# Beginning the stationary operand's tiles at 0, 64, 128 or 192 bytes from the moving operand's, modulo 256, in some visits of a two-matmul feed-forward

## The chip, the cores and the metric

One core of one Trainium2 chip runs the whole program. The metric is the device time of one execution in microseconds; the median of the runs counts. The program uses TensorE (PE; its weight loads are shown apart as PEld), VectorE (DVE), ScalarE (ACT), GpSimd (POOL) and the DMA queue of SyncE (SP).

## The reference

```python
scores = where((rel >= 0) & (rel < 64), q @ k.T / 8, -1e9)   # batch 8, heads 8, 576 positions, 64 wide
x = (softmax(scores) @ v)  ->  4608 tokens x 512
h = x @ w_in                                  # w_in 512 x 2048
g = maximum(h, 0) + alpha * minimum(h, 0)
out = g @ w_out                               # w_out 2048 x 512
```

All arrays are float32.

## The kernel before

The program has an early part and a late part. The early part is the banded attention in tiles of 128 tokens, and the first matmul with w_in, unit by unit of 512 tokens (n = 0 to 8); its g goes out to a scratch in DRAM. The late part, the function `second`, reads g back in quarters and forms the product with w_out by a scheme of Strassen's kind: of four quarters a11, a12, a21, a22 it takes seven sums (numbered by ORDER = 1, 2, 6, 7, 5, 3, 4), multiplies each with a prepared sum of w_out's quarters, and adds the seven products up at the end. There are 9 units times 4 duos of this (u = 0 to 35), so 252 products. One product is called a visit here.

The products are made to nearly float32 precision from two rounded parts of each operand, a high and a low one: high times high, high of g times low of w, low of g times high of w. For each visit ACT writes the high part of g's sum (`ys.u.i.h`, tile yh), DVE subtracts it from the sum to get the low part (`ys.u.i.l`, tile yl), and then PE issues twelve matmuls (`O.u.i`, L721): three pairs of parts, two halves j of the inner dimension, two halves h of the tokens. Each has a stationary operand of 128 columns, a slice of yh or yl, and a moving operand of 256 columns, a slice of wh or wl:

```python
for part, w in ((y_hi, w_hi), (y_hi, w_lo), (y_lo, w_hi)):
    for j in range(2):
        for h in range(2):
            nc.tensor.matmul(banks[bank][:, h * EH:(h + 1) * EH],
                             part[x][:, j * HW + h * P:j * HW + (h + 1) * P],   # stationary: g's sums
                             w[k][:, j * EH:(j + 1) * EH], ...)                 # moving: w_out's sums
```

PE loads the stationary slice of the next matmul while the present matmul streams its moving slice, so both read the same memory, SBUF, at the same time.

yh and yl exist ten times (SLOTS); `new_slot` hands them out in turn, so visit number v of the late part, counted in the order of the program from 0, uses slot v modulo 10.

A planner (`Program.order`) fixes the order of all instructions from costs and due times that are numbers in the code; the tiles' addresses play no part in it.

Where the tiles lie within a partition matters for the change. wh and wl (28 tiles of 512 float32 each) lie in one pool, one behind the other, and so do x's parts xh and xl of the even units (2,048 float32 each), diff, the partial sums and the cells. All these sizes are multiples of 2,048 bytes, so all these tiles begin at the same place modulo 2,048. The pool of the late part follows, and begins at that place too. It opens with a filler, `apart`, of 464 float32 (1,856 bytes, which is seven times 256 and 64 more). Behind it lie yh_0, yl_0, yh_1, yl_1 and so on, and then the tiles for g, 2,048 bytes each. So every yh, yl and g tile begins 64 bytes behind w's tiles modulo 256 (and 320 modulo 512). The slices that the matmuls take begin at multiples of 512 bytes within a tile. In the first matmul (`cell`, L625) the stationary operand is a slice of wh or wl and the moving one a slice of xh or xl; both begin at multiples of 512 bytes in tiles that begin at the same place, so there the two are 0 bytes apart modulo 256. Its unit n = 0 is partly done in halves, with 256 moving columns instead of 512.

Of the kernel before, what the change touches and what calls it, by code (L numbers as in the profile page):

```python
# [9 lines left out]
F32 = mybir.dt.float32  # L10
F32R = mybir.dt.float32r
# [3 lines left out]
ALU = mybir.AluOpType  # L15
# [166 lines left out]
def banded_attention_then_prelu_ffn(  # L182
# [11 lines left out]
    nc = tc.nc  # L194
    P = 128
# [11 lines left out]
    HW = BT * P // 2  # L207
    EH = E // 2
# [11 lines left out]
    w_hi, w_lo = ([const.tile([P, 512], F32R, name=f"w{x}_{k}") for k in range(7 * DUOS)] for x in "hl")  # L220
# [30 lines left out]
    banks = [psum.tile([P, 512], F32, name=f"bank_{i}") for i in range(6)]  # L251
# [8 lines left out]
    def halves_of(*bs):  # L260
        return [f"bank.{b}.{i}" for b in bs for i in range(2)]
# [3 lines left out]
    def add(name, engine, busy, emit, *args, **kw):  # L265
        p.add(name, {engine: (busy, emit)}, *args, **kw)
# [52 lines left out]
    raw_at = [0]  # L319

    def chunk(name, c, f, second, start=0.0):
        r = raw_at[0] % len(raws)
        ulps, k_ulps = ulp_ring[raw_at[0] % 2], f"e.ulps.{raw_at[0] % 2}"
# [100 lines left out]
    def bank_of(i):  # L424
        return banks[i].rearrange("p (e k) -> p e k", e=NP)
# [56 lines left out]
    def value(t, i):  # L482
        av = [bank_of(b).rearrange("p (i a) q -> p i a q", i=2)[:, i] for b in V_BANK]
        pt, at = turned[t % 2].rearrange("p a h u b q -> p a h (u b q)"), 2 * (t % KRING)
        for a in range(2):
            for block, to, from_ in ((1, slice(0, P), slice(W, 3 * W)), (0, slice(0, W), slice(0, W)),
                                     (2, slice(W, P), slice(3 * W, 4 * W))):
                for h in range(2):
                    for x in range(2):
                        r, hs = slice(x * W, (x + 1) * W), slice(h * D, (h + 1) * D)  # L490
                        nc.tensor.matmul(av[x][hs, a, to], vring[r, a, at + block, hs], pt[r, a, h, from_],  # L491
                                         start=block == 1, stop=block == 2)
# [110 lines left out]
    def begin_of(n):  # L603
        return BEGIN + n * CELL * NF
# [35 lines left out]


    y_hi, y_lo, ring = [], [], {"at": 0}

    def new_slot():
        ring["at"] += 1
        return (ring["at"] - 1) % SLOTS

    def fetch_weights(k):
        for at, (kept, key) in enumerate(((w_hi, f"wh.{k}"), (w_lo, f"wl.{k}"))):
# [3 lines left out]
    SETS, SLOTS = 4, 10  # L653
    g_of = []

    def open_late():

        early.close()
        pool = ctx.enter_context(tc.tile_pool(name="late", bufs=1))
        pool.tile([P, 464], F32, name="apart")  # L660
        for i in range(SLOTS):
            y_hi.append(pool.tile([P, 512], F32R, name=f"yh_{i}"))
            y_lo.append(pool.tile([P, 512], F32R, name=f"yl_{i}"))
        g_of.extend([pool.tile([P, 512], F32, name=f"g_{s}_{q}") for q in range(4)] for s in range(SETS))

    bank_ring, slot_of = [0], {}

    def y_keys(x):
        return [f"yh.{x}"], [f"yl.{x}"]

    def second(n):
        acc = {}
        for i in ORDER:
            acc[i] = bank_ring[0] % 8
            bank_ring[0] += 1
        for d in range(DUOS):
            u = n * DUOS + d
            s = u % SETS
            base = begin_of(NB) + 4.0 + u * UNIT
            for q in range(4):  # L680
                add(f"gf.{u}.{q}", "SP", 0.5, lambda s=s, q=q, d=d: nc.sync.dma_start(g_of[s][q].rearrange("p (j t) -> p j t", j=2), hidden[n][d][:, q]),
                    ["late", *(f"far.g.{n}.{d}.{q}.{j}" for j in range(2))], [f"g.{s}.{q}"], service=0.9, earliest=base - 45)

            def cell(q, s=s):
                return lambda: g_of[s][q]

            def both(name, to, a, b, op, reads, writes):
                add(name, "DVE", 0.61, lambda: nc.vector.tensor_tensor(out=to(), in0=a(), in1=b(), op=op), reads, writes)  # L688

            def parts(i, value, ks):  # L690
                x = slot_of[u, i] = new_slot()
                his, los = y_keys(x)
                add(f"ys.{u}.{i}.h", "ACT", 0.54, lambda: nc.scalar.copy(y_hi[x], value()), [*ks, "late"], his)  # L693
                add(f"ys.{u}.{i}.l", "DVE", 0.61, lambda: nc.vector.tensor_tensor(out=y_lo[x], in0=value(), in1=y_hi[x].bitcast(F32), op=ALU.subtract),  # L694
                    [*ks, *his], los)

            a11, a12, a21, a22 = (cell(q) for q in range(4))
            k11, k12, k21, k22 = ([f"g.{s}.{q}"] for q in range(4))
            d_ = lambda: diff
            parts(1, a11, k11)  # L700
            parts(2, a12, k12)
            both(f"z3.{u}", d_, a11, a21, ALU.subtract, [*k11, *k21], ["diff"])
            both(f"z1.{u}", a21, a21, a22, ALU.add, k22, k21)
            both(f"z2.{u}", a11, a21, a11, ALU.subtract, k21, k11)
            parts(6, a11, k11)
            parts(7, d_, ["diff"])
            parts(5, a21, k21)
            both(f"z4.{u}", a12, a12, a11, ALU.subtract, k11, k12)
            parts(3, a12, k12)
            parts(4, a22, k22)  # L710
            for at, i in enumerate(ORDER):
                x, bank = slot_of[u, i], acc[i]

                k = 7 * d + at

                def emit(k=k, x=x, bank=bank, d=d):
                    done = 0
                    for part, w in ((y_hi, w_hi), (y_hi, w_lo), (y_lo, w_hi)):
                        for j in range(2):
                            for h in range(2):  # L720
                                nc.tensor.matmul(banks[bank][:, h * EH:(h + 1) * EH], part[x][:, j * HW + h * P:j * HW + (h + 1) * P],  # L721
                                                 w[k][:, j * EH:(j + 1) * EH], start=d == 0 and not done,
                                                 stop=d == DUOS - 1 and done == 11, skip_group_check=True)
                                done += 1

                add(f"O.{u}.{i}", "PE", STEP, emit, [f"wh.{k}", f"wl.{k}", *y_keys(x)[0], *y_keys(x)[1]], halves_of(bank), key=base + at * STEP)

        def total(name, to, k_to, r, i):
            add(name, "DVE", 0.6, lambda: nc.vector.tensor_tensor(out=to, in0=banks[acc[i]], in1=sums_of[r], op=ALU.add),
                [*halves_of(acc[i]), f"r.{r}"], k_to)  # L730

        def write(m, y, cell):
            at = (n * BT + m * BT // 2) * P
            to = out[at:at + HW, y * EH:(y + 1) * EH].rearrange("(i p) e -> p i e", p=P)
            add(f"out.{n}.{m}.{y}", "SP", 0.5, lambda: nc.sync.dma_start(to, cells[cell].rearrange("p (i e) -> p i e", i=2)),
                [f"cell.{cell}.0", f"cell.{cell}.1"], [], service=0.9)

        add(f"u1.{n}", "ACT", 0.5, lambda: nc.scalar.copy(sums_of[0], banks[acc[1]]), halves_of(acc[1]), ["r.0"])
        total(f"d11.{n}", cells[0], ["cell.0.0", "cell.0.1"], 0, 2)
        write(0, 0, 0)  # L740
        total(f"u2.{n}", sums_of[1], ["r.1"], 0, 6)
        total(f"u3.{n}", sums_of[2], ["r.2"], 1, 7)
        total(f"d22.{n}", cells[3], ["cell.3.0", "cell.3.1"], 2, 5)
        write(1, 1, 3)
        total(f"u4.{n}", sums_of[0], ["r.0"], 1, 5)
        total(f"d12.{n}", cells[1], ["cell.1.0", "cell.1.1"], 0, 3)
        write(0, 1, 1)
        total(f"d21.{n}", cells[2], ["cell.2.0", "cell.2.1"], 2, 4)
        write(1, 0, 2)
# [26 lines left out]
    for k in range(KEPT, 7 * DUOS):  # L776
        fetch_weights(k)
    odd_x = [key for c in range(NP) for part in ("xh", "xl") for key in x_keys(part, 4 + c)]
    add("late", "POOL", 0.0, open_late, (), [*early_keys, *odd_x, "late"])
    for n in range(NB):  # L780
        second(n)
# [49 lines left out]
```

## Time and profile before

| | us |
|---|---|
| median of 3 runs | 869.62 (868.14 to 870.24) |
| the profiled execution, its time | 872.26 |
| its span in the trace | 870.5 |
| PE busy | 856.1 (98%) |
| DVE busy | 686.5 (79%) |
| ACT busy | 441.6 (51%) |
| POOL busy | 203.6 (23%) |

The span is the time from the first to the last instruction of the trace; the profiled execution's own time is 1.8 us longer. Busy PE time counts matmuls that overlap, each with an end that is modelled, so the pace of PE is read from the starts of its matmuls, not from their lengths.

### The profile page before, as it was taken

The numbers are of one execution on the slowest core, as the hardware profiler recorded it, in microseconds if no ns is written. First come the engines' busy times: TensorE is split into PE (matmuls) and PEld (weight loads), VectorE is DVE, ScalarE is ACT, GpSimd is POOL, SyncE is SP. The second block draws the span as 40 slices with busy tenths as digits, with TensorE's granted clock in tenths as the row PEclk, the third lists the DMA queues.
The fourth block names the chain that finished last, engine by engine and source line by source line (L and its number), as shares of the span: only waits on it lengthen the run. The fifth ranks groups of instructions, "written<-read, shape, count | busy, mean of one in ns | idle before, by whom it ended". The sixth has DMA issues, their size and how long they took to land.

```text
span 870.5 us, 21140 instructions
## 1 busy us (share of the span) xinstructions
PE 856.1 (98%) x7888; PEld 772.7 (89%) x7888; DVE 686.5 (79%) x1755; ACT 441.6 (51%) x1118; POOL 203.6 (23%) x192
## 2 busy tenths in 40 slices
PE   7999999999999999999999999999999999999998
PEld 7888888888788787888888899999999999999998
DVE  3967899968987897898685547978788887978783
ACT  4887656564467545545434334444444444444441
POOL 3878525762127327411100000000000000000000
PEclk9999999999999999999999999999999999999999
DMA  6888656644468757755326995545444444545201
GB/s 193 246 257 271 211 185 212 200 155 156 158 223 269 257 160 267 243 173 161 113 98 195 319 339 175 156 120 151 119 137 123 145 135 121 151 117 158 83 27 49
DMA packets 121271, 152.91 MB, mean 176 GB/s; under 512 B 10576, under 2 KB 92496, under 8 KB 121168
## 3 DMA queue, kind: packets, MB, share of 16 engines
q1 hardware_dynamic: 120896, 151.30, 55.0%
q8 instruction: 62, 1.02, 0.5%
q14 instruction: 41, 0.34, 0.1%
q10 hardware_dynamic: 272, 0.26, 0.1%
HBM read 95.95 MB, written 55.57 MB: 174 GB/s over the span
## 4 chain that ended last, share of the span: by engine, by line
PE 72%; DVE 11%; DMA 7%; ACT 4%; issue 3%; POOL 2%; SPq 0%; POOLq 0%; DVEq 0%; ACTq 0%
PE bank L721 41%; PE bank L625 25%; DMA raw<-w_out 4%; DVE pt L468 3%; DVE cell L632 3%; ACT w L451 2%; PE bank L491 2%; DVE pt L470 2%; PE bank L435 2%; DMA wol<-staged 1%; PE bank L293 1%; DVE w L444 1%; PE bank L475 1%; DMA raw<-w_in 1%; ACT cell L631 1%
## 5 line engine op out<-in xcount | busy, mean ns | idle before, releaser
L693 ACT CAST yh<-g 128x512 fp32r<-128x512 f32 x216 | 133.3, 622 | 149.9 <-PE bank L721 98.5
L631 ACT ACTIVATE cell<-bank,alphas 128x512 f32<-128x512 f32 (+1 forms) x148 | 99.7, 674 | 163.0 <-PE bank L625 158.8
L694 DVE TENSOR_TENSOR yl<-g,yh 128x512 fp32r<-128x512 f32 x216 | 147.7, 688 | 30.5 <-ACT yh L693 28.5
L625 PE MATMUL bank<-xh,wh 128*128 128x512 f32 (+1 forms) x592 | 160.7, 393 | 3.3 <-DVE cell L632 2.9
L721 PE MATMUL bank<-wl,yh 128*128 128x256 f32 x1008 | 160.0, 281 | 0.0
L721 PE MATMUL bank<-wh,yh 128*128 128x256 f32 x1008 | 160.0, 281 | 0.0
L721 PE MATMUL bank<-wh,yl 128*128 128x256 f32 x1008 | 160.0, 281 | 0.0
L632 DVE SCALAR_TENSOR_TENSOR cell<-bank,alphas,cell 128x512 f32<-128x512 f32 (+1 forms) x148 | 108.1, 734 | 63.0 <-ACT cell L631 56.0
L625 PE MATMUL bank<-xl,wh 128*128 128x512 f32 (+1 forms) x592 | 155.5, 385 | 0.8 <-DVE xl L559 0.7
L625 PE MATMUL bank<-xh,wl 128*128 128x512 f32 (+1 forms) x592 | 155.0, 384 | 0.0
L721 PEld LDWEIGHTS bank<-wl,yh 128*128 128x128 f32 x1008 | 137.5, 190 | 0.0
L721 PEld LDWEIGHTS bank<-wh,yh 128*128 128x128 f32 x1008 | 136.5, 189 | 0.2
L721 PEld LDWEIGHTS bank<-wh,yl 128*128 128x128 f32 x1008 | 136.4, 189 | 0.0
L625 PEld LDWEIGHTS bank<-xh,wh 128*128 128x128 f32 x592 | 106.0, 188 | 31.1 <-DVE cell L632 9.6
L625 PEld LDWEIGHTS bank<-xl,wh 128*128 128x128 f32 x592 | 109.5, 188 | 23.8 <-DVE xl L559 1.2
L625 PEld LDWEIGHTS bank<-xh,wl 128*128 128x128 f32 x592 | 109.6, 188 | 22.1
L451 ACT ACTIVATE w<-w,nm 128x128 f32<-128x128 f32 x288 | 112.0, 393 | 28.4 <-DVE nm L444 28.2
L460 POOL TENSOR_TENSOR w<-w,rc 128x512 f32<-128x512 f32 x72 | 75.2, 1063 | 140.3 <-DVE rc L456 126.2
L468 DVE STREAM_TRANSPOSE pt<-w 32x256 f32<-32x256 f32 x184 | 80.1, 435 | 7.4 <-POOL w L460 4.4
L688 DVE TENSOR_TENSOR g<-g,g 128x512 f32<-128x512 f32 x108 | 74.2, 687 | 2.4 <-DMA g<-g 0.6
L444 DVE CUSTOM_DVE_ANT_0 w<-bank,masks 128x128 f32<-128x128 f32 x288 | 63.5, 285 | 12.0 <-PE bank L435 11.9
L470 DVE STREAM_TRANSPOSE pt<-w 32x128 f32<-32x128 f32 x184 | 55.7, 303 | 3.8
(62 smaller groups left out, 706.9 us busy)
## 6 DMA issues: line engine op xcount, KB each, us to landing
g<-g SPq DMA_DIRECT2D x144, 256.0 KB, 3.4
g<-cell SPq DMA_DIRECT2D x140, 256.0 KB, 2.9
out<-cell SPq DMA_DIRECT2D x36, 256.0 KB, 2.5
q<-qT SPq DMA_DIRECT2D x35, 256.0 KB, 6.1
raw<-w_in SPq DMA_DIRECT2D x16, 512.0 KB, 5.0
raw<-w_out SPq DMA_DIRECT2D x16, 512.0 KB, 6.5
k<-kT SPq DMA_DIRECT2D x18, 384.0 KB, 5.0
v<-vN SPq DMA_DIRECT2D x18, 384.0 KB, 5.8
```

The lines of the kernel that those rows point to most:

```text
L444: nc.vector.tensor_tensor_reduce(out=of_head(weights[t % 2], g), in0=bank_of(S_BANK[t % 2][x])[:, e].rearrange("p (b k) -> p b k", b=2), i ...
L451: nc.scalar.activation(w, w, AF.Exp, scale=-1.0, bias=least[t % 2][:, g:g + 1], accum_out=sums[:, t % 2, g, 0:1])
L460: nc.gpsimd.tensor_tensor(out=w, in0=w, in1=rc.unsqueeze(1).unsqueeze(3).broadcast_to(list(w.shape)), op=ALU.mult)
L468: nc.vector.transpose(to, w[:, x, j])
L470: nc.vector.transpose(to[:, :, j ^ 1], w[:, x, j, :, j ^ 1])
L625: nc.tensor.matmul(h, w[KEPT + f][:, a * P:(a + 1) * P], v[:, a, half], start=k == a == 0, stop=k == 2 and a == NP - 1, skip_group_check=True)
L631: add(f"sl.{name}", "ACT", 0.13 + 0.46 * part, lambda: nc.scalar.activation(g, h, AF.Copy, scale=slope[:, f:f + 1]), ["signs", *k_h], k_g)
L632: add(f"la.{name}", "DVE", 0.12 + 0.56 * part, lambda: nc.vector.scalar_tensor_tensor(out=g, in0=h, scalar=sign[:, f:f + 1], in1=g, op0=AL ...
L688: add(name, "DVE", 0.61, lambda: nc.vector.tensor_tensor(out=to(), in0=a(), in1=b(), op=op), reads, writes)
L693: add(f"ys.{u}.{i}.h", "ACT", 0.54, lambda: nc.scalar.copy(y_hi[x], value()), [*ks, "late"], his)
L694: add(f"ys.{u}.{i}.l", "DVE", 0.61, lambda: nc.vector.tensor_tensor(out=y_lo[x], in0=value(), in1=y_hi[x].bitcast(F32), op=ALU.subtract), ...
L721: nc.tensor.matmul(banks[bank][:, h * EH:(h + 1) * EH], part[x][:, j * HW + h * P:j * HW + (h + 1) * P], w[k][:, j * EH:(j + 1) * EH], sta ...
```

## The change

The filler `apart` goes. In its place there are three small fillers: 64 bytes ahead of slot 0, 192 bytes ahead of slot 4, 64 bytes ahead of slot 8. The tiles of slots 4 to 7 grow from 512 to 576 float32 (2,304 bytes, nine times 256), and begin 0 bytes from w's tiles modulo 256. The 512 float32 in use lie 16, 32 or 48 float32 further on, by a number that is fixed for each visit. That number is 1 (64 bytes) nearly everywhere. Of each 40 visits, numbers 4, 5, 6 and 7 use 0, 1, 2 and 3, that is 0, 64, 128 and 192 bytes.

Counted over 252 visits: visit numbers that are 4, 6 or 7 modulo 40 leave 64 bytes, seven of each kind, so seven visits at 0, seven at 128 and seven at 192 bytes. The other 231 stay at 64 modulo 256. Slots 0 to 3, 8 and 9 keep their size.

Modulo 512 something else changes too. Before, all parts lay 320 bytes from w's tiles. After, those of slots 0 to 3 lie at 64, those of slots 8 and 9 at 320, and in slots 4 to 7, where the shift is 1, the high parts lie at 320 and the low parts at 64. The tiles for g stay at 64 modulo 256 and 320 modulo 512.

The order of the instructions is the same on all five engines, row for row, and so are the semaphores that each waits for; only addresses differ.

```diff
--- before.py
+++ after.py
@@ -640,10 +640,16 @@
 
 
     y_hi, y_lo, ring = [], [], {"at": 0}
+    SHIFTS = ([(1, 1)] * 4 + [(i, i) for i in range(4)] + [(1, 1)] * 32) * 7
 
     def new_slot():
+
+        at = ring["at"]
         ring["at"] += 1
-        return (ring["at"] - 1) % SLOTS
+        return at % SLOTS, SHIFTS[at]
+
+    def y_of(kept, x, shift):
+        return kept[x][:, 16 * shift:16 * shift + 512] if 4 <= x < 8 else kept[x]
 
     def fetch_weights(k):
         for at, (kept, key) in enumerate(((w_hi, f"wh.{k}"), (w_lo, f"wl.{k}"))):
@@ -657,10 +663,12 @@
 
         early.close()
         pool = ctx.enter_context(tc.tile_pool(name="late", bufs=1))
-        pool.tile([P, 464], F32, name="apart")
         for i in range(SLOTS):
-            y_hi.append(pool.tile([P, 512], F32R, name=f"yh_{i}"))
-            y_lo.append(pool.tile([P, 512], F32R, name=f"yl_{i}"))
+            if i in (0, 4, 8):
+                pool.tile([P, 48 if i == 4 else 16], F32, name=f"step_{i}")
+            size = 576 if 4 <= i < 8 else 512
+            y_hi.append(pool.tile([P, size], F32R, name=f"yh_{i}"))
+            y_lo.append(pool.tile([P, size], F32R, name=f"yl_{i}"))
         g_of.extend([pool.tile([P, 512], F32, name=f"g_{s}_{q}") for q in range(4)] for s in range(SETS))
 
     bank_ring, slot_of = [0], {}
@@ -688,10 +696,10 @@
                 add(name, "DVE", 0.61, lambda: nc.vector.tensor_tensor(out=to(), in0=a(), in1=b(), op=op), reads, writes)
 
             def parts(i, value, ks):
-                x = slot_of[u, i] = new_slot()
+                x, (hi, lo) = slot_of[u, i] = new_slot()
                 his, los = y_keys(x)
-                add(f"ys.{u}.{i}.h", "ACT", 0.54, lambda: nc.scalar.copy(y_hi[x], value()), [*ks, "late"], his)
-                add(f"ys.{u}.{i}.l", "DVE", 0.61, lambda: nc.vector.tensor_tensor(out=y_lo[x], in0=value(), in1=y_hi[x].bitcast(F32), op=ALU.subtract),
+                add(f"ys.{u}.{i}.h", "ACT", 0.54, lambda: nc.scalar.copy(y_of(y_hi, x, hi), value()), [*ks, "late"], his)
+                add(f"ys.{u}.{i}.l", "DVE", 0.61, lambda: nc.vector.tensor_tensor(out=y_of(y_lo, x, lo), in0=value(), in1=y_of(y_hi, x, hi).bitcast(F32), op=ALU.subtract),
                     [*ks, *his], los)
 
             a11, a12, a21, a22 = (cell(q) for q in range(4))
@@ -709,16 +717,16 @@
             parts(3, a12, k12)
             parts(4, a22, k22)
             for at, i in enumerate(ORDER):
-                x, bank = slot_of[u, i], acc[i]
+                (x, (hi, lo)), bank = slot_of[u, i], acc[i]
 
                 k = 7 * d + at
 
-                def emit(k=k, x=x, bank=bank, d=d):
+                def emit(k=k, x=x, bank=bank, d=d, hi=hi, lo=lo):
                     done = 0
-                    for part, w in ((y_hi, w_hi), (y_hi, w_lo), (y_lo, w_hi)):
+                    for part, w in ((y_of(y_hi, x, hi), w_hi), (y_of(y_hi, x, hi), w_lo), (y_of(y_lo, x, lo), w_hi)):
                         for j in range(2):
                             for h in range(2):
-                                nc.tensor.matmul(banks[bank][:, h * EH:(h + 1) * EH], part[x][:, j * HW + h * P:j * HW + (h + 1) * P],
+                                nc.tensor.matmul(banks[bank][:, h * EH:(h + 1) * EH], part[:, j * HW + h * P:j * HW + (h + 1) * P],
                                                  w[k][:, j * EH:(j + 1) * EH], start=d == 0 and not done,
                                                  stop=d == DUOS - 1 and done == 11, skip_group_check=True)
                                 done += 1
```

## Rows read from the trace of the kernel before

**Rows 1.** The page: busy shares, and the granted clock in 40 slices.

```profile
PE 856.1 (98%) x7888; PEld 772.7 (89%) x7888; DVE 686.5 (79%) x1755; ACT 441.6 (51%) x1118; POOL 203.6 (23%) x192
...
PEclk9999999999999999999999999999999999999999
```

**Rows 2.** The chain that ended last, in time: start, length, what.

```profile
479.21 32.66 PE bank L625 x144
511.87 354.76 PE bank L721 x3012
866.66 0.69 DVE cell L729
```

**Rows 3.** Busy us (count) of PE, PEld, DVE, ACT, POOL; clock; DMA share; GB/s.

```profile
520.00:860.00 340.00, 340.00 (x2889) 340.00 (x2889) 274.02 (x426) 149.46 (x245) 0.00 (x0) 1.00 0.43 125
```

**Rows 4.** Waits from 510 us on, longest first: us, times, longest.

```profile
ACT yh L693 <- PE bank L721: 128.7, 152, 2.2
DVE yl L694 <- ACT yh L693: 51.2, 59, 3.0
ACT yh L693 <- DVE yl L694: 26.8, 34, 0.8
ACT r L738 <- PE bank L721: 16.6, 9, 5.5
```

**Rows 5.** The timeline in the late part: start, length, engine, what.

```profile
600.16 0.54 PEld L721 LDWEIGHTS bank<-wh,yl 128*128 128x128 f32 x4
600.28 0.63 PE L721 MATMUL bank<-wh,yl 128*128 128x256 f32 x4
...
600.64 0.54 PEld L721 LDWEIGHTS bank<-wh,yh 128*128 128x128 f32 x4
600.75 0.64 PE L721 MATMUL bank<-wh,yh 128*128 128x256 f32 x4
```

**Rows 6.** The line of the late matmuls: durations in ns, first and last start.

```profile
L721 PEld LDWEIGHTS bank<-wh,yh x1008: 187/188/193, 477.4 to 865.3; 128*128 128x128 f32 x168
L721 PE MATMUL bank<-wh,yh x1008: 280/281/282, 477.6 to 865.4; 128*128 128x256 f32 x168
```

**Rows 7.** PE's timeline, first matmul in halves: 256 moving columns.

```profile
31.66 0.64 PE L625 MATMUL bank<-xl,wh 128*128 128x256 f32 x4
...
34.34 0.64 PE L625 MATMUL bank<-xl,wh 128*128 128x256 f32 x4
...
37.83 0.64 PE L625 MATMUL bank<-xl,wh 128*128 128x256 f32 x4
```

**Rows 8.** PE's timeline, the last matmul of the same three cells.

```profile
32.49 0.28 PE L625 MATMUL bank<-xh,wl 128*128 128x256 f32 x1
...
35.18 0.28 PE L625 MATMUL bank<-xh,wl 128*128 128x256 f32 x1
...
38.66 0.28 PE L625 MATMUL bank<-xh,wl 128*128 128x256 f32 x1
```

**Rows 9.** Forms in the late part: count, busy, mean ns, idle before.

```profile
L694 DVE TENSOR_TENSOR yl<-g,yh 128x512 fp32r<-128x512 f32 x202 | 138.2, 688 | 28.6 <-ACT yh L693 26.8
...
L693 ACT CAST yh<-g 128x512 fp32r<-128x512 f32 x202 | 124.8, 622 | 143.4 <-PE bank L721 95.3 <-DVE yl L694 26.8 <-DVE g L688 13.7
...
L694 DVE TENSOR_TENSOR yl<-diff,yh 128x512 fp32r<-128x512 f32 x34 | 23.4, 689 | 23.7 <-ACT yh L693 23.7
...
L693 ACT CAST yh<-diff 128x512 fp32r<-128x512 f32 x34 | 21.1, 622 | 30.0 <-PE bank L721 29.9
```

## The prediction

> **What bounds the kernel now.** The page comes first: PE is busy 98% of the span, and its granted clock is full, the 2.4 GHz level, in all 40 slices [rows 1]. So neither a lower clock nor an idle PE is there to be won back by addresses. Next I read the chain that ended last, in order of time. Its last long link is 354.76 us of 3,012 late matmuls in one piece, from 511.87 us to the end of PE's work; behind it stands one VectorE instruction and a store [rows 2]. That is 251 of the 252 visits of twelve matmuls. The reader is to see that nothing interrupts it: from 520 to 860 us PE is busy 340.00 of 340.00 us, while DVE is busy 274.02 and ACT 149.46 [rows 3], and the waits of this part are all waits of ACT and DVE, mostly for PE [rows 4]. In this part the pace of PE is therefore the time of the kernel, one to one. The pace is 354.76 / 3,012 = 117.8 ns from one matmul's start to the next, or 1.413 us for a visit.
>
> The timeline shows what overlaps within that pace. The load of a group's stationary slices begins 0.12 us before the group's own matmuls (600.16 and 600.28, 600.64 and 600.75) [rows 5], that is one pace ahead: each load begins as the matmul before it begins, and both read SBUF side by side for the whole matmul. A load is recorded with 187 to 193 ns and a matmul with 280 to 282 [rows 6], so several of each are always under way, and what counts is the distance of starts. If two reads hinder each other depending on where their addresses lie modulo 256, it must show in that distance.
>
> **The change part by part.** No instruction is added, removed or moved, and no wait is added, so there is nothing new to queue behind. What can change is how long an instruction takes.
>
> *ACT and DVE, nothing.* They write and read the shifted parts. The trace has both kinds of address: the inputs g lie 64 bytes from w's place, the input diff lies at w's own place, and the times are the same, 688 and 689 ns for the subtraction, 622 and 622 ns for the copy [rows 9]. Should one cost more all the same, DVE has 340 - 274 = 66 us and ACT 190 us of room in that stretch [rows 3], and ACT waits 128.7 us there for PE [rows 4]. Without that cover, even 0.1 us for each of the 21 shifted visits on both engines would be 4.2 us.
>
> *The seven visits at 0 bytes.* The trace has this case. In the first matmul's cells both operands lie 0 bytes apart modulo 256, and some cells stream 256 columns, as the late visits do. From the first matmul of the second group [rows 7] to the last of the third [rows 8] there are seven distances: 32.49 - 31.66 = 0.83 us, 35.18 - 34.34 = 0.84, 38.66 - 37.83 = 0.83. The sum is 2.50 us for 21 distances, 119.0 ns each, which is 1.2 ns more than 117.8. The rows are rounded to 0.01 us, so each of the three is right to about 1 ns, and their mean is good to less. The roles differ (there w is loaded and x streamed), but a load and a stream read side by side in both. Cost: 7 x 12 x 1.2 ns = 0.10 us.
>
> *The seven visits at 128 and the seven at 192 bytes.* No row has these. The lower bound is the part of a pace that does not go with the number of columns. At 0 bytes 512 columns take 32.66 / 144 = 226.8 ns [rows 2], 256 take 119.0, so a column takes 0.421 ns and 256 take 107.8; what 64 bytes cost beyond that is 10.0 ns. An offset without any hindrance might win that: 168 x 10.0 = -1.7 us over both offsets. The upper bound is a load that cannot overlap the stream at all, 188 ns more for each matmul [rows 6]: 168 x 188 = +31.6 us. Between ends so far apart I take the value of the nearest row, the only other offset that the trace has: 1.2 ns. Cost: 168 x 1.2 = 0.20 us.
>
> The Trainium skill speaks to this in "TensorE: Matmul & The Clock Gate", Part 2, step 1: PE has two independent read ports into SBUF, one for the streamed operand and one for the load, so a load takes no read bandwidth from the running matmul. By that page the offset would cost nothing and the sum would be zero, with 869.6 us. The trace nearly agrees, with 119.0 against 117.8 ns; for 128 and 192 bytes no run here shows it yet.
>
> *All other visits.* Modulo 256 they stay where they were. Modulo 512 the parts of slots 0 to 3 (102 visits, 1,224 matmuls) and the low parts of slots 4 to 7 with shift 1 (79 visits, 4 matmuls each, 316) move from 320 to 64. Together they are 1,540 matmuls. The trace cannot test 64 modulo 512. Bounds as above: -10.0 ns each, 15.4 us won; and upwards the 0-byte price, 1.2 ns each, 1.8 us lost. I take nothing: 0 bytes and 320 bytes modulo 512 differ by only 1.2 ns, and a dependence on 256 bytes would have to lie within so small a difference or just miss both.
>
> **The sum.** 0.10 + 0.20 = +0.3 us. On the profiled execution that is a span of 870.5 + 0.3 = 870.8 us and a time of 872.26 + 0.3 = 872.6. That execution is 2.6 us above the median of 869.62, which comes from runs between 868.14 and 870.24. Put on the median, the forecast is **869.9 us**. About 0.3%, 2.6 us, is what a measurement of this kernel can tell from no change, so the forecast is: no change.
>
> **The rivals.**
>
> *Slower: one of the new offsets collides.* The load's and the stream's addresses meet the same part of the memory on every access, and each of the 12 matmuls of such a visit is stretched. With one such offset there are 84 matmuls, so it decides from 2.6 us / 84 = 31 ns each; with both, from 15.5 ns. A load wholly in series, 188 ns, at one offset gives 84 x 188 = 15.8 us and 885.4 us; half of that gives 877.5. For it speaks that 10 ns of each pace do not go with the columns, so something besides streaming is there, and that no row covers 128 or 192. Against it: the one offset where both addresses are equal costs 1.2 ns, and there, if anywhere, I would look for a collision.
>
> *Faster: what matters is modulo 512.* Then 1,540 matmuls, not 21 visits, move to a new place, and if 64 loses all 10.0 ns of hindrance, the time is 869.6 - 15.4 = 854.2 us. It decides from 1.7 ns a matmul. Against it: with the 0-byte cells at 119.0, nothing in the trace reaches below 117.8.
>
> *Slower by the same route.* 64 modulo 512 would have to cost over 1.7 ns a matmul, more than the 1.2 ns that the trace shows at 0. At 3 ns it would be 4.6 us, 874.2 us.
>
> *The new layout does nothing at all*, since the two reads are independent. That gives 869.6 us and cannot be told from the forecast by time; the pace of the seven 0-byte visits would tell.
>
> **How the numbers follow.** No change that can be told, with or without the 0.3 us: 0.87. A collision at one or two of the new offsets: 0.07. A gain by modulo 512: 0.04. A loss by it: 0.02. So faster by over 0.3%: 0.04, within: 0.87, slower: 0.09. The predicted time is that of the first case. Its lower end is the gain of 1.7 us at 128 and 192 bytes, and a further 0.5 us for the spread of medians: 867.4. The upper end is 2.6 us above the median, to the point where a collision would show: 872.3. Either rival beyond these is left out, with at most 0.13.
>
> **What would show it right or wrong.** The chain's last long link should again be some 3,012 late matmuls in one piece, in 354.8 to 355.4 us. In the timeline a visit should take 1.41 us everywhere; those of slot 4 in every fourth turn of ten should take about 1.43 (12 x 119.0), and those of slots 6 and 7 in the same turns no more than 1.43. The pace of slots 0 to 3 and of 8 and 9 should be equal; if they differ, 512 matters and not 256. The forecast is wrong if a visit at 128 or 192 bytes takes 1.6 us or more, since seven or fourteen of these add up, or if the ordinary visits leave 117.8 ns. A gap in PE's work between 520 and 860 us would be a cost that I have not named.

## The result, and the profile after

The changed kernel takes 859.61 us (median of 4 runs, 858.73 to 860.02), against 869.46 us (868.14 to 870.24) for the kernel before: 0.9882 of it, 95% interval 0.9865 to 0.9898. The forecast was no change, with 869.9 us and a range down to 867.4. The time lies outside the range, on the side that got a chance of 0.04.

The page of the changed kernel, its busy shares and the granted clock (its span is 857.9 us):

```profile
PE 843.9 (98%) x7888; PEld 761.7 (89%) x7888; DVE 683.0 (80%) x1755; ACT 441.4 (51%) x1118; POOL 203.6 (24%) x192
...
PEclk9999999999999999999999999999999999999999
```

As in [rows 1], PE is busy 98% of the span at the full clock. The whole of PE's work got shorter: 843.9 us in place of 856.1. The chain that ended last says where (start, length, what):

```profile
477.08 32.67 PE bank L625 x144
509.74 344.23 PE bank L729 x3012
854.00 0.69 DVE cell L737
```

The last long link answers to the one in [rows 2]. The same 3,012 late matmuls take 344.23 us in place of 354.76: 10.5 us of a span that is 12.6 us shorter. The link of 144 matmuls ahead of it takes 32.67 us, against 32.66. The other 2.1 us lie ahead of the late part, which begins at 509.74 in place of 511.87; that varies from run to run by as much (507.6 to 511.9 in the runs below whose early part is the same).

PE's timeline shows how. These are the first groups of seven visits, numbers 4 to 10 of the late part; a visit's length is the distance to the next row:

```profile
513.82 0.64 PE L729 MATMUL bank<-wh,yh 128*128 128x256 f32 x4
...
515.26 0.63 PE L729 MATMUL bank<-wh,yh 128*128 128x256 f32 x4
...
516.67 0.64 PE L729 MATMUL bank<-wh,yh 128*128 128x256 f32 x4
...
518.10 0.63 PE L729 MATMUL bank<-wh,yh 128*128 128x256 f32 x4
...
519.51 0.62 PE L729 MATMUL bank<-wh,yh 128*128 128x256 f32 x4
...
520.88 0.62 PE L729 MATMUL bank<-wh,yh 128*128 128x256 f32 x4
...
522.24 0.62 PE L729 MATMUL bank<-wh,yh 128*128 128x256 f32 x4
```

Visit 4 (0 bytes) takes 1.44 us, visit 5 (64) 1.41, visit 6 (128) 1.43, visit 7 (192) 1.41. So far this is as forecast. Then visit 8, at 64 bytes like nearly all visits of both kernels, takes 1.37 us, and those behind it 1.36, that is 113.3 ns a matmul. Before, each visit at 64 bytes took 1.413. The second turn with shifted visits, numbers 42 to 49:

```profile
565.75 0.62 PE L729 MATMUL bank<-wh,yh 128*128 128x256 f32 x4
...
567.12 0.62 PE L729 MATMUL bank<-wh,yh 128*128 128x256 f32 x4
...
568.48 0.64 PE L729 MATMUL bank<-wh,yh 128*128 128x256 f32 x4
...
569.91 0.63 PE L729 MATMUL bank<-wh,yh 128*128 128x256 f32 x4
...
571.33 0.64 PE L729 MATMUL bank<-wh,yh 128*128 128x256 f32 x4
...
572.76 0.63 PE L729 MATMUL bank<-wh,yh 128*128 128x256 f32 x4
...
574.17 0.62 PE L729 MATMUL bank<-wh,yh 128*128 128x256 f32 x4
...
575.53 0.62 PE L729 MATMUL bank<-wh,yh 128*128 128x256 f32 x4
```

From 519.51 (visit 8) to 565.75 (visit 42) there are 34 visits in 46.24 us, 1.360 each. Visit 44, at 0 bytes, ends that; visit 45, at 64, takes 1.42 us, the old pace. Visits 46 and 47 follow, and 48 is at 1.36 again. So a visit at 64 bytes has two paces, and it looks as if what went before decides which one; the experiments test that. The prediction had named this sign of being wrong, ordinary visits that leave 117.8 ns. PE had no pause at either pace: before in [rows 3], and here between 523 and 563 us, at the fast pace (busy us and count of PE, PEld, DVE, ACT, POOL; clock; DMA share; GB/s):

```profile
523.00:563.00 40.00, 40.00 (x355) 40.00 (x354) 33.41 (x53) 18.52 (x31) 0.00 (x0) 1.00 0.56 166
```

### The profile page after: what moved, and what is told of

It reads as the page before. It is cut to its first block, busy times and chain, and to the rows that moved or that the text cites. A ratio compares the mean times of both kernels' runs of the same rounds, so it can differ in the third digit from the quotient of the medians.

```text
span 857.9 us, 21140 instructions
## 1 busy us (share of the span) xinstructions
PE 843.9 (98%) x7888; PEld 761.7 (89%) x7888; DVE 683.0 (80%) x1755; ACT 441.4 (51%) x1118; POOL 203.6 (24%) x192
## 4 chain that ended last, share of the span: by engine, by line
PE 78%; DVE 11%; DMA 4%; ACT 3%; issue 3%; POOL 1%; SPq 0%; POOLq 0%; ACTq 0%; DVEq 0%
PE bank L729 40%; PE bank L625 31%; DVE pt L468 3%; DMA raw<-w_out 3%; PE bank L491 3%; DVE cell L632 2%; PE bank L435 2%; DVE pt L470 2%; ACT w L451 2%; DVE w L444 1%; PE bank L475 1%; PE bank L293 1%; DMA v<-vN 1%; DVE xl L559 1%; DVE val L350 1%
## 5 line engine op out<-in xcount | busy, mean ns | idle before, releaser
L729 PE MATMUL bank<-wh,yh 128*128 128x256 f32 x1008 | 156.3, 277 | 0.0
L729 PE MATMUL bank<-wh,yl 128*128 128x256 f32 x1008 | 156.2, 277 | 0.0
L729 PE MATMUL bank<-wl,yh 128*128 128x256 f32 x1008 | 156.1, 277 | 0.0
L729 PEld LDWEIGHTS bank<-wh,yh 128*128 128x128 f32 x1008 | 133.8, 188 | 0.3
L729 PEld LDWEIGHTS bank<-wh,yl 128*128 128x128 f32 x1008 | 133.8, 188 | 0.0
L729 PEld LDWEIGHTS bank<-wl,yh 128*128 128x128 f32 x1008 | 133.7, 188 | 0.0
```

What stands on the lines that cost most here:

```text
L729: nc.tensor.matmul(banks[bank][:, h * EH:(h + 1) * EH], part[:, j * HW + h * P:j * HW + (h + 1) * P], w[k][:, j * EH:(j + 1) * EH], start= ...
```

## The experiments

All kernels compute the whole result, and all ratios are to the kernel before, timed on the same chip in the same rounds. "Link" is the last long link of the chain, the late matmuls. Ratios that lie within one another's intervals are not told apart.

| run | late visits | median us | ratio, 95% interval | link us |
|---|---|---|---|---|
| e1_all64 | new layout, all at 64 | 868.95 | 0.9989 (0.9980 to 0.9999) | 354.76 |
| e2_once | visits 4 to 7 at 0, 64, 128, 192, once | 858.40 | 0.9871 (0.9856 to 0.9886) | 343.14 |
| e3_192once | visit 7 at 192 | 857.47 | 0.9870 (0.9847 to 0.9894) | 343.10 |
| e4_128once | visit 6 at 128 | 857.74 | 0.9863 (0.9848 to 0.9878) | 343.06 |
| e5_twice | visits 4 and 234 at 128 | 859.00 | 0.9859 (0.9843 to 0.9876) | 342.07 |
| e6_zero104 | visit 6 at 128, visit 104 at 0 | 865.01 | 0.9931 (0.9916 to 0.9946) | 349.62 |
| e7_split | all at 64, a matmul of visit 6 split | 858.50 | 0.9858 (0.9842 to 0.9875) | 343.13 |
| e8_x192 | as e5_twice, x at 192 in the first matmul | 864.33 | 0.9921 (0.9902 to 0.9939) | 341.91 |
| e9_split2 | old layout, all at 64, two matmuls split | 856.93 | 0.9866 (0.9844 to 0.9887) | 341.83 |
| e10_all128 | old layout, all at 128 | 876.98 | 1.0085 (1.0067 to 1.0103) | 361.46 |
| e11_all192 | old layout, all at 192 | 869.19 | 1.0001 (0.9989 to 1.0013) | 354.76 |
| e12_all0 | old layout, all at 0 | 877.13 | 1.0090 (1.0072 to 1.0107) | 361.44 |
| f1_split_128 | all at 128, two split | 873.95 | 1.0028 (1.0018 to 1.0039) | 357.65 |
| f2_split_192 | all at 192, two split | 857.94 | 0.9842 (0.9827 to 0.9857) | 341.80 |
| f3_split_0 | all at 0, two split | 877.25 | 1.0065 (1.0048 to 1.0083) | 361.64 |

The link is the better measure here, since it leaves out the early part, which differs by some microseconds from run to run: links begin between 507.63 and 511.91 us in kernels whose early part is the same. Medians are compared by the ratio alone, since the runs were on several chips: e5_twice and e9_split2 have links within 0.24 us and medians 2 us apart, but so has the kernel before on their two chips (871.33 and 869.29).

### The layout, or the shifted visits

The new layout with every visit at 64 bytes:

```diff
-    SHIFTS = ([(1, 1)] * 4 + [(i, i) for i in range(4)] + [(1, 1)] * 32) * 7
+    SHIFTS = [(1, 1)] * 280
```

> The layout of the changed kernel, every visit at 64 bytes. Two paces: at 64 bytes the stream has two lasting paces, 117.8 and 113.3 ns a matmul, and it comes in at 117.8; with no visit at another offset it stays there, so the last long link of the chain is again 354 to 356 us and the time 868 to 871 us. Layout: it is the new places modulo 512 and the grown tiles that give 113.3; then the link is 341 to 345 us and the time 857 to 861 us.

Its chain:

```profile
508.95 354.76 PE bank L729 x3012
```

To the hundredth of a microsecond this is the link of before [rows 2]. So the new places modulo 512 (64 in place of 320), the grown tiles and the fillers do nothing to it by themselves, and my rival by way of 512 bytes falls.

Three kernels keep the turn, or one visit of it, a single time:

```diff
+    SHIFTS = [(1, 1)] * 4 + [(i, i) for i in range(4)] + [(1, 1)] * 272   # e2_once
...
+    SHIFTS = [(1, 1)] * 7 + [(3, 3)] + [(1, 1)] * 272                     # e3_192once
...
+    SHIFTS = [(1, 1)] * 6 + [(2, 2)] + [(1, 1)] * 273                     # e4_128once
```

> Only visits 4, 5, 6 and 7 of the first forty are at 0, 64, 128 and 192 bytes, all later ones at 64. Two paces: the stream stays at 113.3 ns from visit 8 to the end; six turns of about 0.26 us are saved, so the link is 342 to 343 us and the time about 858.0 (857.0 to 859.3). Rival, the pace has to be renewed: it goes back to 117.8 within some visits, and the time is 865 to 870 us.

> One visit alone, number 7, at 192 bytes, 251 at 64. Two paces, and 192 is what moves the stream over: 117.8 ns up to visit 7, 113.3 from visit 8, time about 857.8 (857 to 859). If 128 is what moves it: 117.8 throughout, 868 to 871 us.

> One visit alone, number 6, at 128 bytes, 251 at 64. If 128 bytes moves the stream over: 113.3 ns from visit 7 on, time about 857.8 (857 to 859). If only 192 does: 117.8 throughout, 868 to 871 us. The pace in the visit itself was uneven in the changed kernel (115 to 122 ns), so I expect that 128 may do it, with chances even.

The chains of the three, in this order:

```profile
509.63 343.14 PE bank L729 x3012
```

```profile
508.32 343.10 PE bank L729 x3012
```

```profile
509.53 343.06 PE bank L729 x3012
```

One visit out of 252 is worth 11.7 us of the link. Either of the two does it, and the pace stays for over two hundred visits. The other six turns of the changed kernel cost more than they bring: 344.23 against 343.14. A turn that meets the fast pace takes 5.69 us (568.48 to 574.17) in place of 4 x 1.36 = 5.44.

The pace does not last to the end, though. In all three, as in the changed kernel, it is lost at visit 230. (The changed kernel's last turn, visits 244 to 247, brings it back for the four visits that are left.) The timeline of e4_128once there, DVE's sum and PE's loads among it:

```profile
820.23 0.62 PE L729 MATMUL bank<-wl,yh 128*128 128x256 f32 x4
820.41 0.68 DVE L737 TENSOR_TENSOR cell<-bank,r 128x512 f32<-128x512 f32 x1
...
820.69 0.62 PE L729 MATMUL bank<-wh,yl 128*128 128x256 f32 x4
...
821.21 0.53 PEld L729 LDWEIGHTS bank<-wh,yh 128*128 128x128 f32 x4
821.24 0.71 PE L729 MATMUL bank<-wh,yh 128*128 128x256 f32 x4
...
821.79 0.64 PE L729 MATMUL bank<-wl,yh 128*128 128x256 f32 x4
...
822.26 0.64 PE L729 MATMUL bank<-wh,yl 128*128 128x256 f32 x4
...
822.73 0.63 PE L729 MATMUL bank<-wh,yh 128*128 128x256 f32 x4
```

The groups of four stand 0.46 us apart up to 820.69. The loads for the next visit begin at 821.21, where 821.03 would have kept the pace; DVE had read a bank until 820.41 + 0.68 = 821.09, and the visit writes into a bank that such a sum must have emptied. The trace has a semaphore wait of the loads at 821.1. Behind the wait the groups come 0.55 and then 0.47 us apart, and 0.47 is the old pace, 117.8 ns a matmul. At the slow pace this wait was not there: the kernel before goes through visit 230 at 117.8 ns.

### Moving over again, and back

```diff
+    SHIFTS = [(2, 2) if v in (4, 234) else (1, 1) for v in range(280)]               # e5_twice
...
+    SHIFTS = [{6: (2, 2), 104: (0, 0)}.get(v, (1, 1)) for v in range(280)]           # e6_zero104
```

> Visits 4 and 234 at 128 bytes, all others at 64. The runs with one shifted visit fell back to 117.8 ns at visit 230, after a short wait for a bank. Two paces: 113.3 ns from visit 5 to 229, 117.8 from 231 to 233, 113.3 again from 235; against the run with visit 6 alone that is some 19 visits by 0.053 us, 1.0 us: the link about 342.1 us, the time about 856.7. If the second shifted visit does nothing: 857.6.

> Visit 6 at 128 bytes and visit 104 at 0 bytes, all others at 64. Two lasting paces: the visit at 0 bytes puts the stream back to 117.8 ns, and it stays there from 105 to the end; 125 visits by 0.053 us more than with visit 6 alone, so the link is about 349.7 us and the time about 864.4. Rival, 64 bytes finds its way back to 113.3 by itself: 857.5 to 858.5 us.

The links of e5_twice and of e6_zero104:

```profile
511.91 342.07 PE bank L729 x3012
```

```profile
509.30 349.62 PE bank L729 x3012
```

Both are within 0.1 us of the forecast: 342.1 and 349.7. (The time forecast for e5_twice, 856.7 us, was missed by 2.3; its link begins 2.4 us later than that of e4_128once.) One visit at 0 bytes brings the slow pace back for the 147 visits behind it; 64 bytes does not find its way to the fast pace by itself.

### Without any other address

In e7_split all addresses lie at 64 bytes. One matmul of visit 6 is done as two of 128 columns, which adds one matmul and one load to the program; in e9_split2 the same is done to the kernel before, in visits 0 and 234:

```diff
-    nc.tensor.matmul(banks[bank][:, h * EH:(h + 1) * EH], part[...], w[k][:, j * EH:(j + 1) * EH], ...)
+    ends = (0, EH // 2, EH) if u == 0 and at == 6 and done == 5 else (0, EH)
+    for c0, c1 in zip(ends, ends[1:]):
+        nc.tensor.matmul(banks[bank][:, h * EH + c0:h * EH + c1], part[...],
+                         w[k][:, j * EH + c0:j * EH + c1], ...)
```

> Every visit at 64 bytes, and one matmul of visit 6 done as two of 128 columns, each with its own load. If any break in the rhythm of loads and streams moves the stream over: 113.3 ns from visit 7, time 857 to 859 us. If it needs another distance of addresses: 117.8 ns throughout, 868 to 871 us. I lean to the second, 2 to 1, since a wait of PE brought the slow pace and not the fast one.

PE's timeline of e7_split around the split, which is in the group of five:

```profile
516.13 0.63 PE L731 MATMUL bank<-wh,yl 128*128 128x256 f32 x4
516.60 0.64 PE L731 MATMUL bank<-wh,yh 128*128 128x256 f32 x4
517.07 0.74 PE L731 MATMUL bank<-wl,yh 128*128 128x256 f32 x5
517.64 0.62 PE L731 MATMUL bank<-wh,yl 128*128 128x256 f32 x4
518.10 0.62 PE L731 MATMUL bank<-wh,yh 128*128 128x256 f32 x4
518.55 0.62 PE L731 MATMUL bank<-wl,yh 128*128 128x256 f32 x4
```

Ahead of it the groups stand 0.47 us apart, and behind it 0.45 to 0.46. I had leaned the other way, 2 to 1. The layout is that of e1_all64, whose link is 354.76 us; here the chain has it at 343.13. So another address is not needed: this break in the rhythm of loads and streams is enough.

> The kernel before, addresses untouched, with one matmul of visit 0 and one of visit 234 done as two of 128 columns. If the rhythm alone decides: 113.3 ns from visit 3 on, 117.8 from 230 to 234 at most, 113.3 to the end; the link of late matmuls 341.8 to 342.5 us for 3,014 matmuls, and 12 to 13 us less than the kernel before, about 0.985 to 0.987 of it. If the split works only in the layout of the changed kernel: no difference from the kernel before.

The link of e9_split2:

```profile
508.22 341.83 PE bank L723 x3014
```

This is the kernel before, with two matmuls in two pieces and nothing else, and its link is shorter by 12.9 us. (Both lie in the link, hence 3,014: PE takes visit 1 ahead of the 144 matmuls and visit 0 behind them. The second split found the stream at the fast pace already.) Its visit 230 also had to wait, but here the stream stayed at the fast pace, 0.46 and 0.45 us a group behind the wait:

```profile
819.74 0.71 PE L723 MATMUL bank<-wh,yh 128*128 128x256 f32 x4
820.28 0.62 PE L723 MATMUL bank<-wl,yh 128*128 128x256 f32 x4
820.74 0.62 PE L723 MATMUL bank<-wh,yl 128*128 128x256 f32 x4
821.19 0.62 PE L723 MATMUL bank<-wh,yh 128*128 128x256 f32 x4
```

So a wait is one way back to the slow pace, and not a sure one. All seven kernels with the new layout that came to visit 230 at the fast pace lost it there; e9_split2 and, further below, f2_split_192, both with the old layout, waited too and kept it. Why was not tried.

### The other offsets throughout

Four kernels, or pairs of them, differ in the filler ahead of the late tiles alone: 448, 464, 480 or 496 float32 give 0, 64, 128 and 192 bytes.

```diff
-        pool.tile([P, 464], F32, name="apart")
+        pool.tile([P, 480], F32, name="apart")   # 128 bytes; 496 for 192, 448 for 0
```

> The kernel before with the filler lengthened, so that every visit is at 128 bytes. In the changed kernel such a visit took 119.1 ns a matmul after one at 64, uneven, 115 to 122. If that is its lasting pace: link 357 to 359 us, 3 to 4 us slower than before. If the unevenness was the way to the fast pace: 113.3 to 114 ns, link 341 to 343 us, 12 us faster.

> The kernel before with the filler lengthened, so that every visit is at 192 bytes. A single visit there took 117.6 ns a matmul. If that lasts: link 354 us, no difference from before. If 192 has the fast pace too, as the halves of the first matmul had it with x at 192 bytes (113 to 114 ns): link 341 to 343 us, 12 us faster.

> The kernel before with the filler shortened, so that every visit is at 0 bytes. A visit at 0 took 119.8 ns a matmul, with eleven of twelve distances at 120: link 361 us, 6 to 7 us slower than before. If 0 bytes has a fast pace as well, which the stream finds by itself: under 350 us.

The links at 128, at 192 and at 0 bytes:

```profile
510.18 361.46 PE bank L721 x3012
```

```profile
507.63 354.76 PE bank L721 x3012
```

```profile
509.65 361.44 PE bank L721 x3012
```

The same three with the two split matmuls of e9_split2:

> Every visit at 128 bytes (there 120.0 ns a matmul, 877 us), with one matmul of visits 0 and 234 done as two. If the rhythm alone has two states at any offset: 113.3 ns from visit 3 on, link 342 us, 857 us. If 128 bytes has no fast pace: 120 ns throughout, 876 to 878 us.

> Every visit at 192 bytes (there 117.8 ns a matmul, 869.2 us), with one matmul of visits 0 and 234 done as two. If the rhythm alone has two states at any offset: 113.3 ns, link 342 us, 857 us. If 192 bytes has no fast pace: 117.8 ns throughout, 868 to 870 us. Since a single visit at 192 left the stream at 113.3 behind it, I lean to the first.

> Every visit at 0 bytes (there 120.0 ns a matmul, 877 us), with one matmul of visits 0 and 234 done as two. If the rhythm alone has two states at any offset: 113.3 ns, link 342 us, 857 us. If 0 bytes always collides, as a visit at 0 put a fast stream back to the slow pace: 120 ns throughout, 876 to 878 us. I lean to the second.

```profile
510.95 357.65 PE bank L723 x3014
```

```profile
509.08 341.80 PE bank L723 x3014
```

```profile
508.52 361.64 PE bank L723 x3014
```

Divided by the number of matmuls, with the kernel before and e9_split2 for 64 bytes:

| offset | ns a matmul, undisturbed | ns a matmul, after the split |
|---|---|---|
| 0 | 120.0 | 120.0 |
| 64 | 117.8 | 113.4 |
| 128 | 120.0 | 118.7 |
| 192 | 117.8 | 113.4 |

So both matter. At 64 and at 192 bytes there are two lasting paces. At 0 bytes only one was found. At 128 the split moved the stream by a little over 1 ns and not to the fast pace. Nothing more than the filler and the split differs between these kernels. My lean on f2_split_192 and on f3_split_0 held; f1_split_128 came out between its two cases. e10_all128 fell outside both of its cases (link 357 to 359 us, or 341 to 343): the lasting pace at 128 bytes is slower than the 119.1 ns of a single visit there.

Undisturbed, 0 and 128 bytes are alike and so are 64 and 192, as if the place modulo 128 counted; behind the split 0 and 128 differ by 1.3 ns. That 256 is the right modulus is not shown: e1_all64 tests 64 against 320 modulo 512, and no other pair was tried.

### The first matmul

x's parts were set 192 bytes behind w's. In the first matmul w is loaded and x streamed, so modulo 256 the loaded tile lies 64 bytes behind the streamed one there too, as in the late part:

```diff
+    const.tile([P, 48], F32, name="ahead")
     xs = [[const.tile([P, NP, BT * P], F32R, name=f"x{x}_0") for x in "hl"]]
...
-                pool.tile([P, 48 if i == 4 else 16], F32, name=f"step_{i}")
+                pool.tile([P, {0: 32, 4: 48, 8: 16}[i]], F32, name=f"step_{i}")
```

> As with visits 4 and 234 at 128 bytes, and x's parts of the first matmul begin 192 bytes behind w's modulo 256, so that a load of w there lies 64 bytes ahead of the stream of x, as the late parts lie ahead of w. If the offset matters in the first matmul as in the late one: 512 columns take 220 to 224 ns in place of 226.7, and over 1,680 of these matmuls 4 to 11 us are won: 846 to 853 us. If other engines or the attention set the time of the early part, or if a stream of 512 columns has room for its load: 856 to 857.5 us.

Its last 144 matmuls with 512 columns, and the late ones:

```profile
481.26 33.59 PE bank L626 x144
514.84 341.91 PE bank L730 x3012
```

This was a miss, outside both cases: 33.59 us against 32.65 to 32.69 in the other kernels that have these matmuls in one piece, 233.3 ns a matmul in place of 226.8. The late part is as fast as that of e5_twice, and the whole is slower than it, 864.33 against 859.00 us, on the same chip. The halves, with 256 columns, went the other way:

```profile
33.75 0.62 PE L626 MATMUL bank<-xl,wh 128*128 128x256 f32 x4
34.20 0.62 PE L626 MATMUL bank<-xh,wl 128*128 128x256 f32 x4
```

These two groups stand 0.45 us apart, where 119.0 ns a matmul [rows 7, rows 8] makes 0.48. What is good at 256 columns is not at 512. Why it is worse there was not tried further.

The trace shows one thing more. Here the late part comes in at the fast pace: its first five groups begin at 514.68, 515.14, 515.60, 516.05 and 516.50 us, 0.45 to 0.46 apart, three visits ahead of the first shifted one. In e5_twice, with the same late layout modulo 256, those visits take 117.8 to 118.2 ns a matmul. Modulo 256 only the place of x differs, so the matmuls ahead of the late part also decide at which pace it begins.

## Why the prediction was wrong

*What bounds the kernel* held: late matmuls without a gap, one to one with the time.

*ACT and DVE, nothing* held; the engines follow PE. *No new wait* held only at the old pace: at the fast one PE waits at visit 230 for a bank, and visits 231 to 243 of the changed kernel run at 117.8 ns behind it.

*The 21 shifted visits* came out near the forecast where the stream was at the old pace: 1.43 us was forecast for a visit at 0 bytes and no more than 1.43 for the other two, and 1.44, 1.43 and 1.41 were found. The first turn takes 5.69 us (513.82 to 519.51), 0.04 more than four visits of 1.413; seven of these make the +0.3 us of the sum. In part that is luck: the 0-byte price was too small, 2.2 ns a matmul where it lasts (e12_all0 against before), not 1.2, and the visit at 192 cost nothing. The rows of the halves hold only short runs. Against the fast pace, where five of the seven turns ran, a turn costs 0.25 us.

*All other visits* is the step that failed. "I take nothing" was right of the layout: e1_all64 repeats 354.76 us. It was wrong of the visits themselves, because I held the pace of a visit to depend on its own addresses alone. It depends on what the stream did before as well. A visit at 128 or 192 bytes leaves the visits at 64 behind it at 113.3 ns, one at 0 leaves them at 117.8, and they keep what they get, but for the wait at visit 230. In the changed kernel 192 is always the last of a turn, so nearly all visits between turns are fast, and the link is 10.5 us shorter, with the price of the turns in it.

*"Nothing in the trace reaches below 117.8"*, which I held against a gain, misread [rows 2]. There 512 columns take 226.8 ns, and half of that is 113.4: the fast pace to within 0.1 ns. I drew a line through 119.0 and 226.8 instead, got 107.8 ns for 256 columns and a fixed part of 10.0, and so had a bound that looked unreal. The simpler reading, that 512 columns show the stream without hindrance and that the late matmuls lose 4.4 ns each, gives 3,012 x 4.4 = 13.3 us as the worth of the late part. e9_split2 and f2_split_192 won 12.9 and 13.0 of it. Two matching numbers do not show that the stream alone sets the fast pace; that part is argued.

*The rival by modulo 512* had the right sign and the wrong mechanism. The rival of a collision did not come: the worst lasting offsets cost 2.2 ns a matmul, far from the 15 to 31 that would have decided by themselves.

Moving the loaded tiles by 64 bytes alone changes the lasting pace from 117.8 to 120.0 ns (before and e12_all0). By the rule of the Trainium skill, "TensorE: Matmul & The Clock Gate", Part 2, step 1, a load takes no read bandwidth from the running matmul, so the offset would cost nothing; the measurement decides against that. Whether read bandwidth is what the offset changes, no run shows.

What stays open is the state itself: what in the rhythm of load and stream differs between the two paces. The recorded loads don't tell. In the view of one line's instructions (shortest, median and longest in ns), the loads at 64 bytes and 117.8 ns, then at 192 bytes and 117.8 ns, then at 0 bytes and 120.0 ns:

```profile
L729 PEld LDWEIGHTS bank<-wh,yh x1008: 187/188/192, 474.5 to 862.4; 128*128 128x128 f32 x168
```

```profile
L721 PEld LDWEIGHTS bank<-wh,yh x1008: 187/187/188, 473.2 to 861.0; 128*128 128x128 f32 x168
```

```profile
L721 PEld LDWEIGHTS bank<-wh,yh x1008: 187/192/192, 475.2 to 869.7; 128*128 128x128 f32 x168
```

At 0 bytes most loads last 192 ns, and at 64 bytes some do; but at 192 bytes none does, at the same pace as at 64. It also stays open why the wait at visit 230 threw out some streams and not others, and what 128 bytes does.

## What to carry to other kernels

Where a stream of matmuls with fresh stationary operands runs without a gap, compare its pace per column with the best that the same trace shows for longer moving operands; if it is some per cent worse, a different place of one operand modulo 256, or one matmul done in two pieces, may move the whole stream, and each is a change of a line. Price a disturbance by what it leaves behind as well as by its own length, since here one visit of 1.4 us was worth 11.7 us. Look for the places where the fast pace is lost again, in the starts of the matmuls and not in busy shares, which were 98% in both.

## What was not expected of the hardware

A stream of equal matmuls on addresses that are equal modulo 256 ran at 117.8 or at 113.3 ns a matmul for hundreds of microseconds, at the same granted clock (1.00), and changed from one to the other within one visit. One matmul done as two of 128 columns was enough. At 192 bytes there were the same two paces. Loaded and streamed operands at 0 or 128 bytes from each other modulo 256 had 120.0 ns as their lasting pace when undisturbed. At 512 columns the order was another one: 226.8 ns at 0 bytes, and 233.3 with the loaded operand 64 bytes behind the streamed one.
